# Three changes of order and engine in the attention stage of a two-block kernel

## The chip, the cores and the metric

The kernel runs on one core of a Trainium2 chip. The metric is the device time of one execution in microseconds; the times before are the median of three runs. A profile of one more execution gives the span from its first to its last instruction, and every instruction's start and duration.

## The reference

Two blocks follow each other. The first is linear attention with a decay, in blocks of 64 positions, over q, k and v of shape (batch 4, heads 8, length 768, width 64). The second mixes along the length with a low-rank pair U (768 x 32) and V (32 x 768), adds that to its input, and sends the sum through two dense layers with a relu between them. Cut to what matters:

```python
intra = einsum('bhic,bhjc->bhij', qb, kb) * Dmask      # decay mask
out   = einsum('bhij,bhjd->bhid', intra, vb) + einsum('bhid,bhde->bhie', qb * lam_pow, kv_state)
kv_state = lam_block * kv_state + einsum('bhsd,bhse->bhde', kb * rev_pow, vb)

x = out as (batch, 768, 512)
u = x + (x^T U V)^T                                     # low-rank sum along the length
y = u + relu(u w_ch1) w_ch2                             # 512 -> 2048 -> 512
```

U, V, w_ch1 and w_ch2 arrive as 64-bit floats; the kernel loads them as pairs of 32-bit words and makes 32-bit values of them itself.

## The kernel before

**Attention.** A step `s` handles 128 positions of one batch for all 8 heads; there are 6 steps in a batch and 24 in all, so the batches end with steps 5, 11, 17 and 23. In each step TensorE transposes q and k of the next step into one PSUM tile (`prep`, L358) that ScalarE copies out (L364). It multiplies k by q (`scores`, L406), VectorE multiplies the scores by the decay mask (`masked`, L415), and TensorE multiplies by v (`intra`, L444). TensorE also forms the new key-value product (`state`, L424), in the same PSUM buffer that `prep` uses, and VectorE takes it from there (L430 in a batch's first step, L432 in the later ones, there with ScalarE's faded old state, `fade`, L399). `inter` (L455) adds the part of the old state; ScalarE copies the step's result x out (L461). GpSimd scales q and k (`scale`, L390 and L379).

**The low-rank sum.** After the last step of a batch, TensorE sums U against the batch's six x tiles (`low`, L471) into a tile that shares its PSUM buffer with that of `intra`. ScalarE copies the sum out (L481). VectorE cuts it to its high bits (`low_rows`, L511). Three further pieces follow, each called by one `next_of_low`: `spread`, four ScalarE copies of the high part (L519); `low_part`, two subtractions that leave the low part (L523); `spread_low`, two ScalarE copies of that (L530). High and low parts stand in one tile, `p_hl`, in which TensorE multiplies them by V (`mix`, L551), first the high and then the low columns. VectorE adds the product to x, which makes it u (`mixed`, L563).

**u.** Seven steps after its own, u of a step is complete. It is stored to memory (`store`, L569, one transfer from the SP queue), transposed by TensorE (`turn`, eight L600), and split by VectorE (`split`, L620 and L621) into a high part t and a low part; `turned` lets ScalarE scale the high part (L607) and GpSimd form a third part (L608). The PSUM tile of the transposes is the one in which `mix` of the next step puts its product.

**The weights.** Conversions of U, V and the first two column tiles of w_ch1 from 64 to 32 bits are cut into small pieces (`weight_steps`, `split_steps`, `v_steps`). The dictionary `side` says in which step each piece is asked for, and `aside` runs those of a step: fetches on the SP queue, VectorE's L160, L149, L178, L186, L191, L209, L217 and L224, and ScalarE's L167, L168 and L212. ScalarE's pieces are put into a list that `late` runs in a later place. For V, VectorE's copies of the high part are L695 and the subtractions L699, one pair by VectorE and one pair by GpSimd.

**The order.** In this stage the order is written out by hand. The list `pieces` (L629 to L656) names the pieces of each step in order, and each piece issues its instructions to the queues of its engines, which take them strictly in that order. Nothing reorders them later. The number `done` is the step whose u is made in this step.

**After the attention.** The two dense layers follow as long rows of matrix products (L806, L816, then L939, L941, L943), each written as three products of high and low parts, with the last conversions and the transfers of the middle result beside them.

Of the kernel before, what the change touches and what calls it, by code (L numbers as in the profile page):

```python
# [18 lines left out]
def kernel(  # L19
# [28 lines left out]
    nc = tc.nc  # L48
# [3 lines left out]
    NT = S // P  # L52
# [10 lines left out]
    TG = N // P  # L63
# [5 lines left out]
    FG = (NS - NT - 1) // TG  # L69
# [11 lines left out]
    def on_scalar(what):  # L81
        if late and late[0] is None:
            late.append(what)
        else:
            what()
# [12 lines left out]
    def tmp(name):  # L98
        return wconv.tile([P, C], FP32, tag="tmp", bufs=3, name=name)
# [132 lines left out]
    def w1_steps(ft, in_parts=False, apart=False):  # L232
        def tile_of():
            w1v[ft] = w1_pool.tile([P, 3, C], F32R, tag="w1", name="w1")
            return w1v[ft]

        cols = moe_w_ch1[:, ft * P : (ft + 1) * P].rearrange("(c p) f -> p c f", p=P)
        return split_steps(tile_of, cols, in_parts, apart=apart)
# [244 lines left out]
    def low_rows(b):  # L483

        pp, t = pps.pop(b), tmp("p_h")[0:R]
        own = [(slice(g * R, (g + 1) * R), slice(g * P, (g + 1) * P)) for g in range(G)]
        if b == B - 1:
            h, h2, l, l2 = (p_hl[g * R : (g + 1) * R] for g in range(G))
            for rows, cols in own:
                nc.vector.tensor_scalar(  # L490
                    t[:, cols].bitcast(U32), pp[rows].bitcast(U32), HI, None, ALU.bitwise_and
                )

            def low_part():
                for rows, cols in own:
                    nc.vector.tensor_tensor(
                        out=l[:, cols], in0=pp[rows], in1=t[:, cols], op=ALU.subtract
                    )

            def spread():  # L500
                nc.scalar.copy(h, t)
                nc.scalar.copy(h2, t)

            def spread_low():
                nc.scalar.copy(l2, l.bitcast(FP32))

            pps[b] = [spread, low_part, spread_low]
            return

        rows_f = pp  # L510
        nc.vector.tensor_scalar(t.bitcast(U32), rows_f.bitcast(U32), HI, None, ALU.bitwise_and)  # L511
        wide = [slice(x * 2 * P, (x + 1) * 2 * P) for x in range(2)]

        def place(g, low):
            return p_hl[g * R : (g + 1) * R, wide[low]]

        def spread():
            for g in range(G):
                nc.scalar.copy(place(g, 0), t[:, wide[g // 2]])  # L519

        def low_part():
            for x in range(2):
                nc.vector.tensor_tensor(  # L523
                    out=place(2 * x, 1), in0=rows_f[:, wide[x]], in1=t[:, wide[x]],
                    op=ALU.subtract,
                )

        def spread_low():
            for x in range(2):
                nc.scalar.copy(place(2 * x + 1, 1), place(2 * x, 1).bitcast(FP32))  # L530

        pps[b] = [spread, low_part, spread_low]

    def next_of_low(b):
# [95 lines left out]
    for s in range(NS):  # L630
        b, c = divmod(s, NT)
        done = s - NT - 1
        more = s + 1 < NS
        turns = done > 0 and (done - 1) // TG < FG
        mixes = 0 <= done < NS - NT - 1
        step = [("prep", s + 1), ("scale", s + 1)] * more
        step += [("turn", done - 1)] * turns + [("mix", done)] * mixes
        step += [("mix", done + 1)] * (not more)
        step += [("next_of_low", b - 1)] * (c == 0 and b > 0)
        step += [("fade", s)] * (c == 1)  # L640
        step += [("late", s - 1)] * (s in (NT, 3 * NT - 1))
        step += [("split", done - 1)] * turns + [("next_of_low", b - 1)] * (c == 0 and b > 0)
        step += [("mixed", done)] * mixes + [("mixed", done + 1)] * (not more)
        step += [("next_of_low", b - 1)] * (c == 0 and b > 0)
        step += [("intra", s), ("state", s), ("inter", s)]
        step += [("late", s)] * (s < NT - 1 or s == NT)
        step += [("turned", done - 1)] * (done > 0) + [("late", s)] * (done >= 0)
        step += [("scores", s + 1)] * more
        step += [("low", b)] * (more and c == NT - 1)
        step += [("aside", s)] * (s >= 2 * NT)  # L650
        step += [("masked", s + 1)] * more
        step += [("low_rows", b)] * (more and c == NT - 1)
        step += [("fade", s + 1)] * (more and c > 0)
        step += [("aside", s)] * (s < 2 * NT)
        step += [("store", done)] * (done >= 0 and done // TG < FG)
        pieces += step  # L656
    waiting = {name: list(range(NS)) for name in "qkv"}

# [12 lines left out]
    def v_steps():  # L671

        st = {}

        def dst():
            if "v" not in st:
                st["v"] = wconv.tile([P, C], FP32, tag="wf", name="vf")[0 : 2 * R, 0:SH]
            return st["v"]

        def parts(gs):  # L680
            for half in range(2):
                rows, cols = slice(half * R, (half + 1) * R), slice(half * SH, (half + 1) * SH)
                for g in gs:
                    yield v_hl[g * R : (g + 1) * R, cols], rows

        def five():
            st["t"] = t = wconv.tile([P, C], FP32, tag="wt", name="vt")[0 : 2 * R, 0:SH]
            nc.vector.tensor_scalar(
                t.bitcast(U32), st["v"].bitcast(U32), HI, None, ALU.bitwise_and
            )  # L690
            on_scalar(lambda: high(0))

        def high(g, copy=nc.scalar.copy):
            for out, rows in parts((g,)):
                copy(out, st["t"][rows])  # L695

        def low(g, engine):
            for out, rows in parts((g,)):
                engine.tensor_tensor(  # L699
                    out=out, in0=st["v"][rows], in1=st["t"][rows], op=ALU.subtract  # L700
                )

        halves = [moe_V[:, half * SH : (half + 1) * SH] for half in range(2)]
        return weight_steps(dst, halves, SH, 2 * R, in_parts=True) + [
            five, lambda: low(1, nc.vector), lambda: high(2, nc.vector.tensor_copy),
            lambda: low(3, nc.gpsimd),
        ]
# [5 lines left out]
    side = {}  # L713
    for steps, at in (
        (u_side, (-1, 1, 1, 2, 2)),
        (v_steps(), (0, 0, 3, 3, 4, 4, 4, 5, 4, 5)),
        (w1_steps(0, True), (3, 4, 5, 6, 8, 9, 10, 11, 13, 14, 15)),
        (w1_steps(1, True, True), (8, 9, 10, 11, 16, 17, 19, 20, 21, 22, 23, NS)),
    ):
        assert len(steps) == len(at)  # L720
        for step, n in zip(steps, at):
            side.setdefault(n, []).append(step)
# [67 lines left out]
    turns = iter([0, 0, 0, 0] + [1, 0] * (NG * FT))  # L790
# [69 lines left out]
    c0, b = NS - NT, B - 1  # L860
# [182 lines left out]
```

## Time and profile before

| what | value |
|---|---|
| median of three runs | 676.49 us (675.99 to 676.75) |
| the profiled execution's own time | 676.67 us |
| its span | 674.9 us |
| TensorE busy | 659.7 us, 98% |
| VectorE busy | 500.4 us, 74% |
| ScalarE busy | 280.0 us, 41% |
| GpSimd busy | 111.9 us, 17% |
| attention steps | from the start to about 124 us |

The page gives the busy time of each engine (PE is TensorE, PEld its weight loads, DVE VectorE, ACT ScalarE, POOL GpSimd, SP the queue that issues transfers), the span in 40 slices with a digit for the busy tenths of each, the clock that TensorE was granted, and the chain of work that ended last. A line of the timeline has start, duration, engine, source line, operation, output and input, count, and in square brackets the idle time ahead of it with what ended it. A row of the list of waits has the waiting group, the group waited for, the total in us, the number of waits and the longest.

### The profile page before, as it was taken

The page shows a single profiled execution, that of the slowest core. Times are in us where ns is not written, and L with a number is a line of the kernel's source. Part 1 is how long each engine was busy: PE and PEld are TensorE (multiplying, and loading weights), DVE is VectorE, ACT ScalarE, POOL GpSimd, SP SyncE. Part 2 cuts the span into 40 slices and gives each one's busy share as a digit, 9 for nine tenths or more (in the row PEclk, how much of TensorE's full clock was granted, in tenths as well). Part 3 has the DMA queues.
Part 4 walks back from the last instruction along what each step waited for, and adds up shares of the span by engine and source line. Part 5 has one row for each costly group of instructions (what it writes and reads, how often), then busy time and mean ns, then how long its engine had stood idle before and what let it go on. Part 6 is the DMA issues. An engine that isn't in the chain of part 4 may idle for free.

```text
span 674.9 us, 13392 instructions
## 1 busy us (share of the span) xinstructions
PE 659.7 (98%) x5242; PEld 541.2 (80%) x5242; DVE 500.4 (74%) x864; ACT 280.0 (41%) x534; POOL 111.9 (17%) x92
## 2 busy tenths in 40 slices
PE   8989899999999999999999999999999999999997
PEld 7878788887888888888888888888888888888886
DVE  4778989887999777777798255786586776865864
ACT  3666777554555444444455122332232322322320
POOL 4446666440000000000000000030030200300300
PEclk9989999999999999999999999999999999999999
DMA  9999885164777655555577999945363363443421
GB/s 206 220 216 250 214 218 137 50 226 149 244 267 241 230 203 203 203 203 203 203 252 263 316 315 383 312 169 156 94 203 109 110 200 97 155 157 95 157 92 62
DMA packets 131776, 131.29 MB, mean 195 GB/s; under 512 B 81346, under 2 KB 89794, under 8 KB 131714
## 3 DMA queue, kind: packets, MB, share of 16 engines
q1 hardware_dynamic: 130512, 130.05, 60.8%
q8 instruction: 41, 0.67, 0.4%
q10 hardware_dynamic: 1202, 0.39, 0.2%
q14 instruction: 21, 0.17, 0.1%
HBM read 80.09 MB, written 50.33 MB: 193 GB/s over the span
## 4 chain that ended last, share of the span: by engine, by line
PE 93%; DVE 3%; issue 1%; SPq 1%; ACT 1%; DMA 1%; DVEq 0%
PE pz L806 27%; PE pz L941 13%; PE pz L939 13%; PE pd L816 13%; PE pd L943 13%; PE px L444 3%; PE pss L406 2%; PE px L455 2%; PE pqk L358 1%; PE pkv L424 1%; PE pp L471 1%; SPq L279 1%; DVE vp L523 1%; PE pm L551 1%; DMA qraw<-in_q_dram 1%
## 5 line engine op out<-in xcount | busy, mean ns | idle before, releaser
L806 PE MATMUL pz<-u_hl,w 128*128 128x512 f32 x768 | 190.1, 397 | 0.0
L806 PEld LDWEIGHTS pz<-u_hl,w 128*128 128x128 f32 x768 | 144.0, 188 | 35.2 <-ACT r L812 0.3
L941 PE MATMUL pz<-w_hl,m 128*128 128x512 f32 x384 | 151.1, 396 | 0.0
L939 PE MATMUL pz<-w_hl,m 128*128 128x512 f32 x384 | 150.9, 396 | 0.0
L943 PE MATMUL pd<-w_d,m 128*128 128x512 f32 x384 | 149.5, 396 | 0.0
L922 ACT ACTIVATE m<-mt 128x512 fp32r<-128x512 f32 x96 | 60.6, 632 | 196.3 <-PE pd L943 133.1
L923 DVE SCALAR_TENSOR_TENSOR m<-rm,m 128x512 fp32r<-128x512 f32 x96 | 71.5, 746 | 53.1 <-ACT m L922 52.6
L968 POOL TENSOR_TENSOR o<-o,u 128x512 f32<-128x512 f32 x20 | 29.9, 1528 | 447.4 <-DVE o L964 447.4
L821 DVE SCALAR_TENSOR_TENSOR r<-pd,r 128x512 f32<-128x512 f32 x96 | 61.8, 686 | 53.7 <-ACT r L812 43.5
L816 PE MATMUL pd<-u_d,w 128*128 128x512 f32 x384 | 98.6, 397 | 0.0
L812 ACT ACTIVATE r<-pz 128x512 f32<-128x512 f32 x96 | 52.2, 596 | 93.2 <-PE pz L806 93.1
L941 PEld LDWEIGHTS pz<-w_hl,m 128*128 128x128 f32 x384 | 72.3, 188 | 17.7
L939 PEld LDWEIGHTS pz<-w_hl,m 128*128 128x128 f32 x384 | 72.3, 188 | 17.6
L943 PEld LDWEIGHTS pd<-w_d,m 128*128 128x128 f32 x384 | 72.3, 188 | 17.6
L816 PEld LDWEIGHTS pd<-u_d,w 128*128 128x128 f32 x384 | 72.1, 188 | 17.3
L924 DVE SCALAR_TENSOR_TENSOR m<-m 128x512 fp32r<-128x512 f32 x96 | 69.1, 721 | 0.9
L921 DVE TENSOR_SCALAR mt<-rm 128x512 uint32<-128x512 uint32 x96 | 46.1, 481 | 27.1 <-DMA rm<-r_d 26.4
L415 DVE TENSOR_TENSOR sm<-pss,mask 128x512 f32<-128x512 f32 x48 | 30.8, 684 | 10.1 <-PE pss L406 10.0
L212 ACT CAST w<-wt 128x512 fp32r<-128x512 f32 x32 | 19.9, 621 | 30.5 <-DVE wt L209 23.4
L444 PE MATMUL px<-vraw,sm 128*64 128x64 f32 x768 | 29.3, 230 | 0.9 <-ACT faded L399 0.7
L390 POOL TENSOR_TENSOR qs<-qt,powq 128x512 f32<-128x512 f32 x20 | 26.1, 1306 | 23.2 <-ACT qt L364 22.4
L444 PEld LDWEIGHTS px<-vraw,sm 128*64 128x64 f32 x768 | 26.1, 141 | 4.3 <-ACT faded L399 0.9
(96 smaller groups left out, 677.1 us busy)
## 6 DMA issues: line engine op xcount, KB each, us to landing
r_d<-r SPq DMA_DIRECT2D x96, 256.0 KB, 2.5
rm<-r_d SPq DMA_DIRECT2D x96, 256.0 KB, 2.7
words<-in_moe_w_ch_dram SPq DMA_DIRECT2D x30, 512.0 KB, 4.2
w_d<-w SPq DMA_DIRECT2D x16, 768.0 KB, 3.3
w_hl<-w_d SPq DMA_DIRECT2D x16, 512.0 KB, 6.6
vraw<-in_v_dram SPq DMA_DIRECT2D x24, 256.0 KB, 4.1
u_d<-x_nat SPq DMA_DIRECT2D x24, 256.0 KB, 3.5
u<-u_d SPq DMA_DIRECT2D x24, 256.0 KB, 4.0
```

The lines of the kernel that those rows point to most:

```text
L444: nc.tensor.matmul(out=px[half[t], x, a, :], lhsT=sm[:, x, a, half[t]], rhs=vr[:, 2 * a + x, :], start=(a == 0), stop=(alone and a == HP - 1),
L806: nc.tensor.matmul(out=acc[g][0], lhsT=w[:, n, ct, :], rhs=uhl[g][:, n, ct, :], start=(ct == 0 and n == 0), stop=(ct == CT - 1 and n == 1),)
L812: nc.scalar.mul(rs[g], acc[g][0], 4096.0 + 1.0)
L816: nc.tensor.matmul(out=acc[g][1], lhsT=w[:, 2, ct, :], rhs=ud[g][:, ct, :], start=(ct == 0), stop=(ct == CT - 1),)
L821: nc.vector.scalar_tensor_tensor(rs[g], acc[g][1], 4096.0, rs[g], ALU.mult, ALU.add)
L921: nc.vector.tensor_scalar(t.bitcast(U32), r.bitcast(U32), HI, None, ALU.bitwise_and)
L922: nc.scalar.activation(out=m[:, 0], in_=t, func=AF.Relu)
L923: nc.vector.scalar_tensor_tensor(m[:, 1], r, 0.0, hi, ALU.max, ALU.subtract)
L924: nc.vector.scalar_tensor_tensor(m[:, 2], hi, E, low, ALU.mult, ALU.subtract)
L939: nc.tensor.matmul(out=pz, lhsT=m[:, 0, cols], rhs=hl[:, 0], start=first, stop=False)
L941: nc.tensor.matmul(out=pz, lhsT=m[:, 1, cols], rhs=hl[:, 1], start=False, stop=end)
L943: nc.tensor.matmul(out=pd, lhsT=m[:, 2, cols], rhs=dd, start=first, stop=end)
```

## The change

There are four edits, three of them in the list of pieces.

- `low_part` of batches 0 to 2 runs on GpSimd instead of VectorE.
- In the last step of batches 1 and 2 (steps 11 and 17, `early`), `store` and `turn` of the step's own u come ahead of `low`, and its `split` right behind `masked`. Before, `turn` and `split` came at the head of the next step. In the first step of a batch (`rows`), `scale` comes after `mix`, `spread` and `low_part`, and `spread_low` comes after `inter` and `turned` instead of before `intra`.
- From s = 7 on, `aside` comes ahead of `masked`. Before, it did so from s = 12.
- One piece of V's conversion, VectorE's copy of the high part (L695), moves from step 4 to step 5.

```diff
         def low_part():
             for x in range(2):
-                nc.vector.tensor_tensor(
+                nc.gpsimd.tensor_tensor(
                     out=place(2 * x, 1), in0=rows_f[:, wide[x]], in1=t[:, wide[x]],
                     op=ALU.subtract,
                 )
...
-        step = [("prep", s + 1), ("scale", s + 1)] * more
-        step += [("turn", done - 1)] * turns + [("mix", done)] * mixes
+        rows = c == 0 and b > 0
+        early = c == NT - 1 and more and done >= 0
+        step = [("prep", s + 1)] * more
+        step += [("turn", done - 1)] * (turns and not rows) + [("mix", done)] * mixes
         step += [("mix", done + 1)] * (not more)
-        step += [("next_of_low", b - 1)] * (c == 0 and b > 0)
+        step += [("next_of_low", b - 1)] * rows + [("next_of_low", b - 1)] * rows
+        step += [("scale", s + 1)] * more
         step += [("fade", s)] * (c == 1)
         step += [("late", s - 1)] * (s in (NT, 3 * NT - 1))
-        step += [("split", done - 1)] * turns + [("next_of_low", b - 1)] * (c == 0 and b > 0)
+        step += [("split", done - 1)] * (turns and not rows)
         step += [("mixed", done)] * mixes + [("mixed", done + 1)] * (not more)
-        step += [("next_of_low", b - 1)] * (c == 0 and b > 0)
         step += [("intra", s), ("state", s), ("inter", s)]
         step += [("late", s)] * (s < NT - 1 or s == NT)
         step += [("turned", done - 1)] * (done > 0) + [("late", s)] * (done >= 0)
+        step += [("next_of_low", b - 1)] * rows
         step += [("scores", s + 1)] * more
+        step += [("store", done), ("turn", done)] * early
         step += [("low", b)] * (more and c == NT - 1)
-        step += [("aside", s)] * (s >= 2 * NT)
+        step += [("aside", s)] * (s > NT)
         step += [("masked", s + 1)] * more
+        step += [("split", done)] * early
         step += [("low_rows", b)] * (more and c == NT - 1)
         step += [("fade", s + 1)] * (more and c > 0)
-        step += [("aside", s)] * (s < 2 * NT)
-        step += [("store", done)] * (done >= 0 and done // TG < FG)
+        step += [("aside", s)] * (s <= NT)
+        step += [("store", done)] * (done >= 0 and done // TG < FG and not early)
...
-        (v_steps(), (0, 0, 3, 3, 4, 4, 4, 5, 4, 5)),
+        (v_steps(), (0, 0, 3, 3, 4, 4, 4, 5, 5, 5)),
```

## The prediction

> **What bounds the kernel now.** I read the page first. TensorE is busy 98% of the span and makes 93% of the chain that ended last; its weakest slices all lie in the first fifth.
>
> ```profile
> span 674.9 us, 13392 instructions
> PE   8989899999999999999999999999999999999997
> PEclk9989999999999999999999999999999999999999
> PE 93%; DVE 3%; issue 1%; SPq 1%; ACT 1%; DMA 1%; DVEq 0%
> ```
>
> So only TensorE's idle time can be won. The busy times by stretches of 20 us put it: 16.98, 18.48, 17.34, 17.78, 19.66 and 18.42 us in the first six, 108.7 of 120 us, then 20.00 of 20 in each stretch from 140 on. Nearly all of its idle time, 11.3 us, lies in the attention steps. Second view, the waits between 40 and 230 us, longest first:
>
> ```profile
> PE pqk L358 <- DVE kv L430: 5.3, 3, 2.1
> ...
> PE pqk L358 <- DVE kv L432: 1.0, 1, 1.0
> ```
>
> Three waits of L358 for L430: one behind the low-rank sum of each of the batches 0, 1 and 2 (steps 7, 13, 19). The fourth, for L432, is in step 9. Third view, the timeline round the second of these:
>
> ```profile
> 66.58 1.52 PE L471 MATMUL pp<-x_nat,u_w 128*32 128x128 f32 x48
> 68.16 1.06 ACT L481 COPY p_f<-pp 32x128 f32<-32x128 f32 x4 [1.42 <-PE pp L471]
> 69.60 0.67 DVE L191 SCALAR_TENSOR_TENSOR wf<-m,sc 128x512 f32<-128x512 f32 x1
> 70.20 1.66 ACT L519 CAST vp<-p_h 32x256 fp32r<-32x256 f32 x4
> 71.37 1.05 POOL L379 TENSOR_TENSOR ks<-kraw,small 128x512 f32<-128x512 f32 x1
> 71.51 1.63 DVE L523 TENSOR_TENSOR vp<-p_f,p_h 32x256 fp32r<-32x256 f32 x2
> 72.79 0.85 ACT L530 CAST vp<-vp 32x256 fp32r<-32x256 f32 x2 [0.92 <-DVE vp L523]
> 73.78 0.41 DVE L430 COPY kv<-pkv 128x256 f32<-128x256 f32 x1
> 74.25 0.46 PE L358 MATMUL pqk<-ident,qraw 64*128 64x64 f32 x8 [2.06 <-DVE kv L430]
> 75.44 1.15 PE L444 MATMUL px<-vraw,sm 128*64 128x64 f32 x32
> ```
>
> L430 frees the bank that the next q and k transposes (L358) write. It is late because VectorE, in order, first does L191, the split of u (L620, L621), L523 and L563. The first L523 took 1.19 us, the second 0.42: the first stood behind GpSimd's L379. Fourth view, stretches of 1 us round the first boundary (columns: PE, PEld, DVE, ACT and POOL busy, granted clock, DMA share, GB/s):
>
> ```profile
> 41.00:42.00 1.00, 0.00 (x0) 0.00 (x0) 0.94 (x3) 0.89 (x3) 0.15 (x1) 1.00 0.26 59
> 42.00:43.00 1.00, 0.62 (x18) 0.62 (x18) 1.00 (x3) 0.89 (x2) 0.00 (x0) 0.91 0.96 248
> 43.00:44.00 1.00, 1.00 (x14) 0.78 (x14) 0.71 (x2) 0.69 (x2) 0.03 (x1) 0.50 1.22 275
> ```
>
> After the 1.70 us of idle there the clock stood at 0.50 from about 42.8 to 46.1. L444 took 1.97 us against 1.15, and L444 to the next L406 was 3.3 us against 2.2 in step 19: with the mix of u ahead of it the halving cost about 1.3 us.
>
> **What the Trainium skill says.** "SBUF — State Buffer", section "SBUF: two separate sides": VectorE (two SBUF inputs, or a two-port mode) and GpSimd share one port pair, an exclusive lock held for a whole instruction. The trace agrees: 1.19 against 0.42 us. "TensorE: Matmul & The Clock Gate", "What's actually happening": the clock is halved after an idle window of about 3.4 us that runs freely. The trace has 3.3 us at 0.50; but the idle of 2.06 and 1.58 us at the other boundaries did not trip it, so where idle time falls counts as well as its length. "GPSIMD Engine Reference", "Performance versus the Vector engine": GpSimd is some 2 times slower on two-input operations. Here 128x512 is 1.27 us (L390) against VectorE's 0.69.
>
> **Part 1: the low part by GpSimd.** The trace has no 32x256 instruction there; the nearest, L699 on GpSimd (32x384, the same subtraction), takes 1.01 to 1.09. By columns I take 0.70 each; bounds: 0.42 (VectorE's) and 1.27 (L390). VectorE loses 2 x 0.42 plus the lock's 0.8. GpSimd does the two first, then qs (1.27) and ks (1.05); at the second boundary it is ready at 69.95 and L390 then ends near 72.7, before inter at 75.7 needs it. ScalarE's order changes: L461 and L607 now stand ahead of the two L530.
>
> **Part 2: u's transposes ahead.** For u of steps 4 and 10 the eight L600 leave the head of the next step for the place ahead of L471. Eight of them hold up what follows by 0.24 (68.52 to 68.76), so L471 and all behind it is 0.24 later. L600 waits for L563, with L471 and so L481 queued behind it: L563 ended at 66.74 against the scores' end at 66.64, and with L186 gone from ahead of it (part 5) ends 0.6 earlier. Its L620 and L621 (0.7 each) then fill VectorE's idle 1.27 ahead of L511. The store's one DMA passes one weight fetch in SP's queue in step 11; neither is read within 20 us (the fetched words first at 91.79): nothing.
>
> **Part 3: the second and third boundary, summed.** From the start of L481, by the rows above: L364 at 1.09, L519 at 2.04, L461 at 3.72, L607 at 4.20, L530 at 4.75, its end at 5.60, and L551's last two matmuls and L444 at about 5.8 (5.7 to 6.0). GpSimd's part is done at 1.65 + 1.40 = 3.05: ahead of L530. L430 comes at about 3.0, so L358 no longer waits. What is late next is L530, in ScalarE's queue.
> - second: L481 at 68.16 + 0.24 = 68.40, L444 at 74.2 against 75.44: -1.2 (1.0 to 1.35).
> - third: L481 at 98.13 + 0.24 = 98.37, L444 at 104.2 against 104.93: -0.7 (0.5 to 0.9).
> Later steps follow rigidly: at the second boundary ScalarE ends L364 and L399 (1.07 each) at 74.0 + 2.1 = 76.1, and the next L461 is not due before TensorE's 76.4; L432 ends at 76.5, and the next L358 is due at 77.3; and from 124 on TensorE has no idle time that would take the gain up.
>
> **Part 4: the first boundary.** No u is ready, so no transposes move. But the new place 5 of V's copy (L695, two, 32x384) moves it from ahead of L415, where nothing waited, to ahead of L430. VectorE's queue at L511's end (38.11) is L699, L699, L695, L695, L430; GpSimd's is L523, L523, L390, L379, and the lock alternates as it did before. Ends: L699 38.67, L523 39.25, L699 39.65, L523 40.25, L695 40.45, L390 41.6, L695 41.8, L430 42.25, against 42.32: 0.0. If L695 passes twice in a row: -1.1 for L358, but L551 waits for L530 until 42.8, so -0.4; at 1.27 for each L523: +1.1. The halved clock: the idle time remains 1.6 to 1.7, so I leave it (else -1.3).
>
> **Part 5: conversions ahead of the masks, steps 8 to 11** (aside's place from s = 7; nothing is due at 7). L160 and L149 (0.4 each alone; L149 took 1.49 behind L390 at 54.04) fall into VectorE's idle 0.76 ahead of L415 at 52.50, which starts 0.15 later. L432 then comes at 55.9 instead of 57.45, and L358's wait of 1.0 goes. But L424 (60.41) writes the bank that L364 reads, and ScalarE runs from L461 at 55.93 through L607, L167, L168, four L399 and two L364 to 60.32 without a gap: unchanged. The wait moves to L424: 0.0 (+0.1 to -0.3). L178, L186 and L191, one each, lie in idle time of VectorE and cost nothing; without it 0.7 each. L191 leaves the place ahead of L620, which part 3 counts.
>
> **Sum**: -1.2 - 0.7 + 0.0 + 0.0 = -1.9 on the span of 674.9, that is 673.0; 1.8 lie around it, so 674.8 for the profiled execution's 676.67. That one stood 0.2 above the median of the runs: 674.6 us.
>
> **Rivals.**
> - The clock too: the first boundary's idle time no longer trips the halving: 674.6 - 1.3 = 673.3. For it: 1.58 did not trip, 1.70 did. Against: I find 1.64.
> - The gain is taken up: ScalarE, which I find the next limit, is later than summed (L461 to L607 was 0.61 at the boundaries, 0.48 elsewhere), or GpSimd at 1.27 adds 1.1 at the first boundary: a gain of some 0.8, 675.7. Within the 0.2% (1.35 us) that a measurement of this kernel can tell.
> - Slower: GpSimd's L523 takes far longer than its columns say. Each 0.1 us costs 0.2 in the first boundary's L430; from 1.75 each L530 waits too, at both others. The gain is gone at 1.65 each; at 2.3 it costs 3.2 + 1.0 + 1.0 less the 1.9 won: 679.8. Against: 1.09 was the most for half as many columns again.
> - Nothing moves: excluded for the order of instructions, which differs on all five queues.
>
> **How the numbers follow.** Forecast 0.45 (its own range 674.0 to 675.2), clock too 0.2, taken up 0.25, slower 0.1. Of the forecast 0.42 and all of the second are beyond 0.2%, and some of the third: faster 0.65, same 0.25, slower 0.1. The range reaches over the clock case below and the taken-up case above: 673.0 to 676.4.
>
> **What would show it.** Right: L358 no longer waits for L430 in steps 13 and 19, L551 waits there for L530, u's split stands ahead of L511, L523 on GpSimd is near 0.7, and L424 of step 10 is still at about 60.4. Wrong: L523 above 1.2; L444 of step 13 less than 0.8 earlier; or a stretch at half clock somewhere new, which would put up to 1.7 us against a gain of 1.9.

## The result, and the profile after

The changed kernel takes 674.32 us (median of 10 runs, 673.45 to 675.56) against 676.11 us of the kernel before on the same chip (10 runs, 674.03 to 676.75). The ratio is 0.9979, with a 95% interval of 0.9967 to 0.9991: wholly below 1, but on both sides of the 0.2% that the prediction took as its mark. The profiled execution took 673.84 us. These are its lines of the page that answer to those shown of before; line numbers of the code are unchanged up to the list of pieces and 5 higher behind it (L695 is L700 now, L699 is L704).

```profile
span 672.0 us, 13396 instructions
PE   8988999999999999999999999999999999999997
PEclk9999999999999999999999999999999999999999
PE 94%; DVE 2%; issue 1%; SPq 1%; ACT 1%; DMA 1%; DVEq 0%
```

The slice of the clock that stood at 8 is gone, and VectorE's share of the chain fell from 3% to 2%. Next, TensorE's own waits between 40 and 230 us, which is the whole list for that engine (the group, what it waited for, the total in us, the number, the longest):

```profile
PE pkv L424 <- issue: 1.8, 2, 1.3
PE pqk L358 <- DVE kv L430: 1.4, 1, 1.4
PE pm L551 <- DVE u_hl L621: 0.8, 2, 0.4
PE pm L551 <- ACT vp L530: 0.3, 1, 0.3
PE px L444 <- issue: 0.3, 1, 0.3
PE px L455 <- issue: 0.2, 1, 0.2
```

L358 waited three times for L430, 5.3 us in all; one wait of 1.4 is left, at the first boundary. The wait for L432 is gone, and L424 has one of 1.3 instead. New are two waits of L551 for u's split (L621), which I had not named, and one for L530, at the third boundary, which I had. At the second boundary the wait for L530 doesn't stand in the list; there it lies within L551's four products, which take 0.96 us from 71.58 on, against 0.48 at the same place before. The second boundary's timeline shows the order that this comes from:

```profile
66.40 1.06 ACT L481 COPY p_f<-pp 32x128 f32<-32x128 f32 x4 [1.70 <-PE pp L471]
...
66.61 0.69 DVE L621 TENSOR_TENSOR u_hl<-pm,ut 128x512 fp32r<-128x512 f32 x1
...
67.36 0.51 PE L551 MATMUL pm<-vp 64*128 64x256 f32 x4 [0.38 <-DVE u_hl L621]
...
68.06 1.52 POOL L523 TENSOR_TENSOR vp<-p_f,p_h 32x256 fp32r<-32x256 f32 x2 [1.98 <-DVE p_h L511]
...
69.99 0.42 DVE L430 COPY kv<-pkv 128x256 f32<-128x256 f32 x1 [1.36 <-PE pkv L424]
...
70.87 0.41 PE L358 MATMUL pqk<-ident,qraw 64*128 64x64 f32 x8
...
71.28 0.83 ACT L530 CAST vp<-vp 32x256 fp32r<-32x256 f32 x2
...
72.47 1.15 PE L444 MATMUL px<-vraw,sm 128*64 128x64 f32 x32
```

VectorE is early now: it idles 1.36 us before L430, and L358 has no bracket. From L481 to L444 it takes 6.07 us, where it took 7.28. I compare kernels by stretches, from one step's first L406 (the scores) to another's; a stretch without a boundary shows what varies for other reasons. Times in us from the two profiled executions, and from a repeat of the changed kernel:

| stretch, by the step whose scores start and end it | before | after | after, repeated |
|---|---|---|---|
| 6 to 8, with the first boundary | 13.07 | 11.63 | 11.60 |
| 8 to 12 | 18.49 | 19.04 | 18.50 |
| 12 to 14, second boundary | 12.13 | 11.16 | 11.16 |
| 14 to 18 | 17.85 | 18.45 | 17.85 |
| 18 to 20, third boundary | 11.64 | 11.16 | 11.15 |

The boundaries gave 1.44, 0.97 and 0.49. The first of these includes a full clock where before had a halved one. The changed kernel's profiled execution lost 0.5 in each of the two stretches between, in short pauses that have no releaser in the trace; the repeat does not have them, so they are not the change's.

### The profile page after: what moved, and what is told of

It is laid out like the page before. It is cut to its first block, busy times and chain, and to the rows that moved or that the text cites. A ratio compares the mean times of both kernels' runs of the same rounds, so it can differ in the third digit from the quotient of the medians.

```text
span 672.0 us, 13396 instructions
## 1 busy us (share of the span) xinstructions
PE 659.3 (98%) x5242; PEld 540.7 (80%) x5242; DVE 494.5 (74%) x858; ACT 280.3 (42%) x534; POOL 115.1 (17%) x98
## 4 chain that ended last, share of the span: by engine, by line
PE 94%; DVE 2%; issue 1%; SPq 1%; ACT 1%; DMA 1%; DVEq 0%
PE pz L811 27%; PE pz L946 13%; PE pz L944 13%; PE pd L821 13%; PE pd L948 13%; PE px L444 3%; PE pss L406 3%; PE px L455 2%; PE pkv L424 1%; PE pqk L358 1%; SPq L279 1%; PE pm L551 1%; PE pp L471 1%; DMA qraw<-in_q_dram 1%; PE pm L600 1%
## 5 line engine op out<-in xcount | busy, mean ns | idle before, releaser
L415 DVE TENSOR_TENSOR sm<-pss,mask 128x512 f32<-128x512 f32 x48 | 30.9, 685 | 12.1 <-PE pss L406 11.8
L444 PE MATMUL px<-vraw,sm 128*64 128x64 f32 x768 | 28.4, 226 | 1.1 <-issue 0.7
L406 PE MATMUL pss<-qt,kt 64*128 64x128 f32 x384 | 28.9, 291 | 0.0
L444 PEld LDWEIGHTS px<-vraw,sm 128*64 128x64 f32 x768 | 25.1, 138 | 4.3 <-issue 0.8
```

Of the source, the lines that this page charges most:

```text
L406: nc.tensor.matmul(out=pss[:, x, a, :], lhsT=kt[half[x], a, :], rhs=qt[half[x], a, :], start=True, stop=True,)
L444: nc.tensor.matmul(out=px[half[t], x, a, :], lhsT=sm[:, x, a, half[t]], rhs=vr[:, 2 * a + x, :], start=(a == 0), stop=(alone and a == HP - 1),
```

## The experiments

My theory: at the second and third boundary it is the order in the queues that counts, above all what stands ahead of L530 on ScalarE; VectorE has slack there. Rivals: what moved the time is VectorE's lighter load (L523 gone to GpSimd), or the transposes put ahead, or the earlier conversions, or the clock alone. Each set of runs has its own runs of the kernel before, with medians of 676.24 to 676.45 us. Where I give an execution's mean clock: one stretch of 3.4 us at 0.50 makes it 0.996 or 0.997 (so in six profiled executions), none leaves it at 0.999 or 1.0 (so in eight); that 0.994 or 0.995 is two such stretches follows by the same sum, but no trace shows it. I call such a stretch a fall of the clock.

The changed kernel itself has ratios of 0.9979 and 0.9971 in two sets of runs, so the times alone don't tell its variants apart where they differ by 0.001 or less. What is said of such differences rests on the stretches, each from one profiled execution; between the changed kernel and its repeat the second and third stretch agree to 0.01 us.

### The changed kernel again, and one part of it undone in each of three

**The same kernel again**, with a blank line in the source:

> The changed kernel once more, with nothing changed, as the measure for the other three and to see what of its profile repeats itself. Theory 1 (ScalarE's queue up to L530 now sets the second and third boundary): the stretch from the first L406 of the scores of step 12 to that of step 14 is 11.2 us again, that from step 18 to step 20 11.2 too, because nothing in them is left to chance. Stretches are named so below: second and third stretch; the first is step 6 to step 8 (11.6 in the profile of the changed kernel, 13.1 before). The idle times of TensorE that no semaphore explains (0.3 us each ahead of the end of L455 in steps 11, 16 and 17 of the changed kernel, 1.2 us in step 2 of the kernel before) should lie elsewhere or be gone if they have nothing to do with the change (theory A), or be at the same places if the change makes them (theory B). Time 674.3 us, 673.5 to 675.5.

674.27 us (22 runs), ratio to before 0.9971 (0.9960 to 0.9982); the stretches are in the table above. Of the 22 executions ten had a mean clock of 0.996 or 0.997 and a median of 675.1; that of the other twelve is 673.6. So the clock still falls in some executions of the changed kernel, and a fall costs about 1.5 us by these medians.

**L523 back on VectorE:**

```diff
-                nc.gpsimd.tensor_tensor(
+                nc.vector.tensor_tensor(
                     out=place(2 * x, 1), ...
```

> The changed kernel with the low part (L523) back on VectorE, all else as changed. Theory 1: at the second and third boundary VectorE has time to spare. L523 starts at L511's end, its second half stands behind L390 and ends some 1.8 us later, L563 and L430 follow, and L430 ends at about 70.8 where the scores ahead of L358 end at 71.0. Second and third stretch stay at 11.2 us. At the first boundary the queue of VectorE gets longer by 0.65 us, L358 waits 2.0 us instead of 1.4, and the clock is halved there in most executions: first stretch 12.3 at full clock, 13.6 with the halving. Whole: 0.6 to 1.9 us slower than the changed kernel, all of it in the first stretch. Theory 2 (VectorE's queue sets all three boundaries, and taking L523 off it is the gain): second and third stretch longer by 0.8 each, first by 1.6: 3 us slower than the changed kernel, that is, slower than before.

675.48 us, ratio 0.9994 (0.9979 to 1.0009). Second stretch 11.15, third 11.17: no loss. First stretch 13.82, with the clock halved. The second boundary of this kernel, from the timeline:

```profile
71.17 1.83 DVE L523 TENSOR_TENSOR vp<-p_f,p_h 32x256 fp32r<-32x256 f32 x2
...
73.64 0.41 DVE L430 COPY kv<-pkv 128x256 f32<-128x256 f32 x1
...
74.11 0.46 PE L358 MATMUL pqk<-ident,qraw 64*128 64x64 f32 x8 [0.46 <-DVE kv L430]
...
74.43 0.83 ACT L530 CAST vp<-vp 32x256 fp32r<-32x256 f32 x2
```

L358 does wait for L430 again, 0.46 us, but L530 ends only at 75.26 and L551 needs it, so that the wait costs nothing. GpSimd's part is worth something at the first boundary alone, where L358 waits 2.50 without it (1.70 in the repeat of the changed kernel with it). That wait is longer by 0.8 us, and falls of the clock are more frequent (seven executions of 14 with one, two with two, as against ten of 22 with one); at 1.43 us for a fall that makes some 1.3 us, as an estimate, where the median is 1.2 above the repeat's.

**The transposes, split and store of u back at the old place:**

```diff
-        early = c == NT - 1 and more and done >= 0
+        early = False
-        step += [("turn", done - 1)] * (turns and not rows) + [("mix", done)] * mixes
+        step += [("turn", done - 1)] * turns + [("mix", done)] * mixes
-        step += [("split", done - 1)] * (turns and not rows)
+        step += [("split", done - 1)] * turns
```

> The changed kernel with u's transposes, their split and the store of steps 11 and 17 back at their old place in the next step; the order of the low-rank sum's pieces, GpSimd's low part and the conversions stay as changed. Theory 1: the move costs time. L471 and L481 come 0.24 us earlier, with them all of ScalarE's queue up to L530, and L551 of the old product no longer waits for L621. L430 is due at about 70.2, ahead of the 71.0 at which L358 could start. Second and third stretch 10.9 us each: 0.5 us faster than the changed kernel. Theory 2: L620 and L621 behind L511 put 1.4 us back into VectorE's queue ahead of L430, L358 waits again: second and third stretch 11.7 to 11.9, 1.0 to 1.4 us slower than the changed kernel.

673.81 us, ratio 0.9961 (0.9944 to 0.9978), although its profiled execution had the clock halved. Second and third stretch 10.91 each, 0.25 less than in the changed kernel. The second boundary:

```profile
70.65 0.42 DVE L430 COPY kv<-pkv 128x256 f32<-128x256 f32 x1
...
71.17 0.41 PE L358 MATMUL pqk<-ident,qraw 64*128 64x64 f32 x8
...
72.63 0.80 PE L551 MATMUL pm<-vp 64*128 64x256 f32 x2 [0.37 <-ACT vp L530]
```

L430 ends at 71.07, and L358 again has no wait. So, with L523 on GpSimd, to put the transposes ahead is a loss by the stretches: it makes L481 0.24 us later, as worked out, and the time that the split leaves free on VectorE nobody needs. The two parts relieve VectorE twice: with L523 on VectorE and the split ahead, as in the run before this one, the boundaries were no slower either. No run takes both away and keeps the new places of `scale` and `spread_low`, so it isn't shown what these two are worth without any relief of VectorE.

**The conversions behind the masks again in steps 7 to 11:**

```diff
-        step += [("aside", s)] * (s > NT)
+        step += [("aside", s)] * (s >= 2 * NT)
...
-        step += [("aside", s)] * (s <= NT)
+        step += [("aside", s)] * (s < 2 * NT)
```

> The changed kernel with the conversions ahead of the masks only from step 12 on, as before. Theory 1: nothing changes. L358 of step 9 waits some 1.0 us for L432 again, but L424 of step 10 waits for ScalarE's L364 either way. From the scores of step 8 to those of step 12 it takes 19.0 us in the profile of the changed kernel (18.5 before), of which 0.3 to 0.5 are idle times that no semaphore explains; here 18.5 to 19.1. L191 stands between L511 and L563 again, which makes L430 of the second boundary 0.7 later, still ahead of L358: second stretch 11.2. Theory 2: that stretch of four steps gets longer by the wait of 1.0, and the second stretch by 0.7.

674.9 us, ratio 0.9975 (0.9965 to 0.9986). The stretch 8 to 12 is 18.50 with and without this edit: the wait only moves, as predicted. But the second stretch is 11.62, which the expectation does not have. The timeline ahead of that boundary has it:

```profile
64.10 0.75 DVE L186 SCALAR_TENSOR_TENSOR sc<-words,sc 128x512 uint32<-128x512 uint32 x1
...
66.10 0.68 DVE L563 TENSOR_TENSOR x_nat<-pm,x_nat 128x512 f32<-128x512 f32 x1
...
66.92 0.47 PE L600 MATMUL pm<-ident,x_nat 64*128 64x64 f32 x8 [0.24 <-DVE x_nat L563]
```

L186 is again ahead of the split and of L563, L563 ends at 66.78, and the transposes, which now stand ahead of L471, wait for it. L481 starts 3.39 us after the scores instead of 2.92. Part 2 of the prediction (the transposes ahead) makes TensorE wait for L563, and part 5 (the conversions ahead of the masks) brings L563's end forward; part 2 without part 5 costs 0.46 more at this boundary.

### ScalarE's order, V's copy, and the clock

**The two L530 ahead of L461 and L607:**

```diff
+        step += [("next_of_low", b - 1)] * rows
         step += [("intra", s), ("state", s), ("inter", s)]
...
         step += [("turned", done - 1)] * (done > 0) + [("late", s)] * (done >= 0)
-        step += [("next_of_low", b - 1)] * rows
```

> The changed kernel with the two L530 put ahead of L461 and L607 in ScalarE's queue, at all three boundaries; nothing else moves on any engine. Theory A (the order in ScalarE's queue up to L530 sets L444): L530 follows L519 directly, at about 70.1 and 99.7 instead of 71.28 and 100.88; L551 no longer waits for it, and L444 comes 0.45 (second) and 0.65 (third) earlier. But the two L364 behind are no earlier, since the same work stands ahead of them, and L424, which writes their bank, then waits for L364: L424 is only 0.2 earlier at each. Second and third stretch 10.95 each against 11.16, first 11.6 or a little less, time -0.4 against the changed kernel. Theory B (only the order matters, L424 waits for nothing): 10.7 and 10.5, time -1.1. Theory C (L530 does not hold TensorE at all): 11.16 and 11.16, time unchanged.

673.67 us, ratio 0.9961 (0.9948 to 0.9974), second and third stretch 11.00 and 11.01: theory A's size. Its second boundary:

```profile
70.00 0.83 ACT L530 CAST vp<-vp 32x256 fp32r<-32x256 f32 x2
...
71.49 1.01 PEld L444 LDWEIGHTS px<-vraw,sm 128*64 128x64 f32 x32 [0.30 <-ACT x_nat L461]
71.49 1.15 PE L444 MATMUL px<-vraw,sm 128*64 128x64 f32 x32
...
73.11 0.69 PE L424 MATMUL pkv<-vraw,ks 128*64 128x64 f32 x16 [0.47 <-ACT kt L364]
```

L551 no longer waits for L530, L444 starts 5.22 us after L481 (66.27) instead of 6.07, and L424 gives most of it back by its wait for L364. L530 was the limit for L444, and ScalarE's whole sum up to the second L364 is the next limit, 0.2 us behind. The wait of 0.30 of L444's weight loads (PEld) for L461 I had not foreseen.

**V's copy (L700) back at step 4**, the rest as changed:

```diff
-        (v_steps(), (0, 0, 3, 3, 4, 4, 4, 5, 5, 5)),
+        (v_steps(), (0, 0, 3, 3, 4, 4, 4, 5, 4, 5)),
```

> The changed kernel with V's copy L695 (L700 here) back at step 4, that is ahead of L415 in VectorE's queue and no longer ahead of L430. Theory A (my part 4: the copy, under the lock with GpSimd, is what keeps L430 late, and ScalarE's L530 at 41.07 to 41.9 is the next limit): L430 starts near 38.8, L358's wait of 1.4 at the first boundary goes, L551 waits for L530 instead, and L444 of step 7 starts at 42.2 against 42.27. First stretch 11.5 against 11.6 at full clock, time -0.1; what is idle is cut in two pieces by L358, so the halved clock should be no more frequent. Rival B (VectorE's queue alone sets this boundary): L444 near 41.3, first stretch 10.7, time -0.9. Rival C (the copy has nothing to do with L430): L430 stays at 40.75, nothing moves.

673.62 us, ratio 0.9964 (0.9951 to 0.9978). The first boundary of this kernel, and then that of the changed kernel (both from the timeline):

```profile
38.39 0.42 DVE L430 COPY kv<-pkv 128x256 f32<-128x256 f32 x1
...
39.14 0.41 PE L358 MATMUL pqk<-ident,qraw 64*128 64x64 f32 x8
...
40.53 0.83 ACT L530 CAST vp<-vp 32x256 fp32r<-32x256 f32 x2
...
40.98 0.81 PE L551 MATMUL pm<-vp 64*128 64x256 f32 x2 [1.01 <-ACT vp L530]
```

```profile
36.58 0.41 DVE L511 TENSOR_SCALAR p_h<-p_f 32x512 uint32<-32x512 uint32 x1 [1.28 <-ACT p_f L481]
...
37.03 1.55 DVE L704 TENSOR_TENSOR vp<-vf,vt 32x384 fp32r<-32x384 f32 x2
37.08 2.09 POOL L523 TENSOR_TENSOR vp<-p_f,p_h 32x256 fp32r<-32x256 f32 x2 [1.90 <-DVE p_h L511]
...
38.59 2.13 DVE L700 CAST vp<-vt 32x384 fp32r<-32x384 f32 x2
...
40.75 0.42 DVE L430 COPY kv<-pkv 128x256 f32<-128x256 f32 x1
...
41.23 0.46 PE L358 MATMUL pqk<-ident,qraw 64*128 64x64 f32 x8 [1.37 <-DVE kv L430]
```

With the copy ahead of L415, L430 comes 1.6 us after L511's end instead of 3.8, L358 does not wait, and L551 waits for L530 in its stead. The first stretch is 11.30 (theory A: 11.5; B: 10.7), 0.30 less than in the repeat of the changed kernel. None of its nine executions had a mean clock below 0.999, against ten below it of the repeat's 22. The kernel before, with its idle time filled and so at full clock, takes 11.64 for this stretch (the next two runs). So without V's copy the change would gain 0.34 there, and its fourth edit takes all but 0.04 of that back.

**The idle time filled, in the kernel before:**

```diff
-        step = [("prep", s + 1), ("scale", s + 1)] * more
+        step = [("busy", 5)] * (s == 7) + [("prep", s + 1), ("scale", s + 1)] * more
...
```

> The kernel before with five 128x128 matmuls of zeros (L343's) added at the head of step 7, in TensorE's queue right ahead of the L358 that waits 1.70 for L430; they compute nothing that is used and fill that idle time. Theory A (the idle of 1.70 there trips the halving, and the halving costs 1.3 to 1.4): the clock stays at 1.00 through the first stretch, which becomes 11.7 against 13.07; second and third stretch unchanged at 12.1 and 11.6; time 1.3 below the kernel before, 675.0, if most executions of the kernel before are halved. Rival B (the halving has another cause, such as the burst of transfers at 42 to 44): clock at 0.50 after 42.8 as before, first stretch 13.1, time as before or up to 0.3 more.

The profiled execution did as theory A has it: 1.38 us of L343 in the idle time, clock 1.00, first stretch 11.64. The transfers, rival B, are excluded as a cause by themselves: from 42 to 47 us they took a share of 1.08 to 1.13 here, at full clock, and 0.96 to 1.22 in the kernel before. The median did not do as theory A has it: 676.11 against 676.24 us, ratio 1.0000 (0.9987 to 1.0013), and ten of 14 executions had a mean clock of 0.997. So this kernel was run once more.

> The kernel of the filled idle time a second time, for its records: of its 14 executions ten had a mean clock of 0.997, although the profiled one had none halved up to step 19. Theory A (the halving goes to another idle place when the first is filled): in an execution at 0.997 the stretch at 0.50 lies behind the wait of 2.06 at the second boundary (about 74 to 78) or the 1.58 at the third. Rival B: it lies in the first stretch as before, filled or not. Rival C: it lies somewhere past the attention steps. If this execution is again without a halved stretch, nothing follows.

676.32 us, ratio 1.0005 (0.9994 to 1.0015); 13 of 18 executions at 0.996 or 0.997, the profiled one among them. Stretches of 1 us at its second boundary (busy of PE, PEld, DVE, ACT and POOL, granted clock, transfer share, GB/s):

```profile
72.00:73.00 1.00, 0.23 (x6) 0.23 (x8) 1.00 (x3) 0.95 (x3) 0.00 (x0) 1.00 0.47 108
73.00:74.00 1.00, 1.00 (x28) 0.98 (x24) 0.91 (x2) 0.83 (x2) 0.50 (x1) 0.81 1.18 321
74.00:75.00 1.00, 1.00 (x18) 0.80 (x16) 0.66 (x1) 1.00 (x4) 1.00 (x2) 0.50 0.60 180
```

The first stretch is again 11.64 at full clock, and now the second is 13.59 instead of 12.12: the halving has gone behind the wait of 2.06 at the second boundary and costs 1.47 there. Theory A holds in this execution: with one idle time filled, the halving came behind the next.

**The same five matmuls in the changed kernel**, at the head of its step 7:

> The changed kernel with the same five matmuls of zeros at the head of step 7, where L358 waits 1.37 for L430. Theory A (what halves the clock in some ten of 22 executions of the changed kernel is this idle time, and its boundaries two and three no longer have one that could): all executions at a mean clock of 0.999 or 1.0, the median as that of its undisturbed executions, 673.6 to 673.9, first stretch 11.6. Rival B (the halving only moves, as it seemed to in the kernel before): still a third or more of the executions at 0.997 and the median at 674.3.

673.69 us, ratio 0.9967 (0.9957 to 0.9978), first stretch 11.61, and all 21 executions at 0.999 or 1.0. In the changed kernel, then, the halving hangs on the first boundary's idle time and on no other in these runs. The median is 0.6 us below the repeat's, a difference that the two ratios (0.9967 and 0.9971) don't establish. Its list of waits also gives a name to the wait of step 10 that the changed kernel's list puts down to "issue":

```profile
PE pkv L424 <- ACT kt L364: 1.3, 1, 1.3
```

### One part alone

**Only L523 moved to GpSimd, in the kernel before:**

```diff
-                nc.vector.tensor_tensor(
+                nc.gpsimd.tensor_tensor(
                     out=place(2 * x, 1), ...
```

> The kernel before with one edit alone: L523 on GpSimd. With the old order of the step L523 stands behind L390 and L379 in GpSimd's queue. Theory A (the place in the queues decides, not which engine): at the second boundary L430 comes at 72.2 instead of 73.78 and L358 at 72.65 without a wait, but GpSimd reaches the two L523 only after L379, at 72.4, and ends them at 73.9; L530 ends at 74.75 instead of 73.64, and L551, which waits for it, lets L444 start at 75.1 against 75.44. Second and third stretch 11.8 and 11.3 (before 12.13 and 11.64); at the first boundary GpSimd is at L523 at 41.15 and L530 ends at 43.4, so 0.0 to 0.5 later there. Time as before, +-0.4. Rival B (VectorE's load was what held the boundaries): L444 1.2 and 0.9 earlier, stretches 10.9 and 10.7, time 674.2 or less.

677.18 us against 676.31, ratio 1.0012 (1.0000 to 1.0024): slower, if anything. First stretch 13.48 with the clock halved, second 12.38 (before 12.13), third 12.25 (before 11.64). The second boundary:

```profile
71.78 1.05 POOL L379 TENSOR_TENSOR ks<-kraw,small 128x512 f32<-128x512 f32 x1
...
72.51 0.41 DVE L430 COPY kv<-pkv 128x256 f32<-128x256 f32 x1
72.80 1.52 POOL L523 TENSOR_TENSOR vp<-p_f,p_h 32x256 fp32r<-32x256 f32 x2
...
74.80 0.38 PE L551 MATMUL pm<-vp 64*128 64x256 f32 x1 [0.41 <-ACT vp L530]
...
77.03 0.69 PE L424 MATMUL pkv<-vraw,ks 128*64 128x64 f32 x16 [0.46 <-ACT kt L364]
```

L430 comes 3.95 us after L481's start (68.56) instead of 5.62, as VectorE's load would have it, and yet it is no gain: L523 stands behind L390 and L379 in GpSimd's queue, L530 waits for it, and L551, L444 and L424 follow. Theory A's mechanism, but I had expected the stretches at 11.8 and 11.3; the waits of L444 for L461 and of L424 for L364, both behind the late L530 on ScalarE, were not in that sum. Together with L523 back on VectorE, above, this decides between the two: the new order without GpSimd gives both later boundaries in full, GpSimd without the new order gives none.

**The mix of steps 5 and 11 ahead of L358:**

```diff
-        step += [("turn", done - 1)] * (turns and not rows) + [("mix", done)] * mixes
+        step += [("turn", done - 1)] * (turns and not rows) + [("mix", done)] * (mixes and not rows)
...
-        step += [("low", b)] * (more and c == NT - 1)
+        step += [("low", b)] * (more and c == NT - 1) + [("mix", done + 1)] * early
```

> The changed kernel with the mix of steps 5 and 11 (four L551) put right behind L471 on TensorE, ahead of the two L358, so that it no longer stands behind u's split on VectorE, which reads the same bank (its wait of 0.38 for L621 at 66.98 to 67.36, which I had not foreseen). Nothing else moves. Theory A (that wait holds L444 of the boundary's step, but TensorE waits later for L530 anyway, whose time is set by ScalarE): L551's wait for L621 goes, L444 of the boundary's step comes about 0.3 earlier, the wait of L551 for L530 in the next step grows by as much, and the second and third stretch stay at 11.15, the time at 674.3. Rival B (the wait is on the path): both stretches 10.8, time -0.7.

674.44 us, ratio 0.9974 (0.9963 to 0.9984); second and third stretch 11.39 and 11.40. Both theories missed. L551 waits no more, but mix and split use one PSUM tile, and now the split waits for the mix. The second boundary:

```profile
67.16 0.69 DVE L620 TENSOR_SCALAR ut<-pm 128x512 uint32<-128x512 uint32 x1 [0.93 <-PE pm L551]
67.89 0.69 DVE L621 TENSOR_TENSOR u_hl<-pm,ut 128x512 fp32r<-128x512 f32 x1
68.49 0.41 DVE L511 TENSOR_SCALAR p_h<-p_f 32x512 uint32<-32x512 uint32 x1
...
68.93 1.66 ACT L519 CAST vp<-p_h 32x256 fp32r<-32x256 f32 x4
```

The split stands ahead of L511 on VectorE, so L519, and with it L530, is 0.24 us later. Of the two possible waits the one that I had overlooked was the cheaper.

### A better version

**What the runs above point to, together:** transposes back, V's copy back, L530 ahead of L461, and u's L607 and L608 of the boundary's step behind the two L364.

```diff
         step += [("scale", s + 1)] * more
+        step += [("turned", done - 2)] * (c == 1 and done > 1)
...
-        step += [("turned", done - 1)] * (done > 0) + [("late", s)] * (done >= 0)
+        step += [("turned", done - 1)] * (done > 0 and not rows) + [("late", s)] * (done >= 0)
```

> A combination meant to beat both: the changed kernel with the transposes, split and store of u back at their old place (as in the third of the earlier experiments), V's copy back at step 4, L530 ahead of L461 and L607, and u's L607 and L608 of the boundary's step behind the two L364 instead of ahead. Theory A (ScalarE's queue up to L530, then its L364, set the boundary): L444 and L424 both come 0.6 to 0.7 earlier than with the transposes back alone, where the stretches were 10.91: second and third 10.2 to 10.3; first 11.1 to 11.3 at full clock; time 672.1 to 672.6 against 674.3 of the changed kernel. Rival B (the rest of TensorE's idle at the boundaries comes from elsewhere): second and third stay at 10.9, time 673.8.

672.64 us (6 runs), ratio to before 0.9948 (0.9931 to 0.9965): faster than the kernel before, and probably than the changed one (0.9971, 0.9960 to 0.9982), though the intervals touch. No execution's mean clock was below 0.999. First stretch 11.16, third 10.12, as theory A has them. The second is 11.29, not 10.2. Up to L455 it agrees with the third to 0.01 us; then this profiled execution has a pause without a releaser in the middle of L455, like those in the table of the result:

```profile
74.43 0.69 PE L455 MATMUL px<-kv,qs 64*64 64x64 f32 x30 [0.84 <-issue]
```

## Why the prediction was right

The forecast was 674.6 us and "faster"; the median is 674.32. What removed the waits and what became the next limit was foreseen; that the total fits so closely is in part luck, as the part on the clock's share shows.

- **Part 3, the size of the gain.** Right in mechanism, a little high: -0.97 and -0.49 in place of -1.2 and -0.7, 1.46 for 1.9. L444 follows L481 by 6.07 at the second boundary where the sum had 5.8. Up to L607 the sum is right to 0.01 (4.21 after L481 for 4.20). Two of its terms are too small: L607 to L530 took 0.67 where it has 0.55, and from the end of L530 to L444 it took 0.36 where it has 0.2, because L551's last product starts only behind the second L530. To that extent the first half of the rival "taken up", a ScalarE that is later than summed, is what happened. That L530 "is late next", in ScalarE's queue, is shown by the runs with L530 moved ahead and with L523 back on VectorE.
- **Part 1.** L523 took 0.72 each without company (1.52 for two, with the gap between them) and 0.93 to 1.09 beside VectorE's L704, where I had 0.70 with bounds of 0.42 and 1.27. I credited GpSimd with clearing VectorE; the runs show that with the split ahead this is worth nothing at the later boundaries, because L551 waits for L530 anyway, and that alone it costs (0.25 and 0.61 us at these two).
- **Part 2.** The price of 0.24 on L481 is right (0.25 per boundary in the run with the transposes back). That they would fill VectorE's idle time is right, but of no use once L523 is on GpSimd. Not foreseen: the split ahead of the mix makes L551 wait 0.38 for L621. It lies within what TensorE later waits for L530 (without it, in the run with the transposes back, the boundary is shorter by L481's 0.24 and no more), and the run with the mix ahead shows that the other order is dearer.
- **Part 4, the waits.** Right: L430 started 3.76 us after L511's end, where the sum has 3.72 (from 38.11 to the start at 41.83), and at full clock the first stretch is 11.60 to 11.63 against 11.64 of the kernel before with its idle time filled. V's copy is what holds L430, as worked out.
- **Part 4, the clock.** Half wrong: I left the halving in, as a thing that is there or not. The runs show it as a thing of chance, in each execution anew. My reading that the 2.06 and 1.58 "did not trip it, so where idle time falls counts" came from a single execution; in the filled kernel the 2.06 did. (The halved stretch is also 3.4 us long, not 3.3: the clocks of its slices in the prediction's fourth view and the 0.50, 0.50 and 0.89 of those up to 47 give 42.8 to 46.2.)
- **The clock's share of the total.** Of all 174 executions of the kernel before in the four sets of runs, 56 had no fall, 95 one and 23 two, 0.81 each; of the changed kernel's 32, 20 had none and 12 one, 0.38 each. At 1.43 each (13.07 less 11.64) that is, as an estimate, 0.6 us that the change wins besides. 1.46 and 0.6 make 2.1, against 1.8 and 2.0 measured in the two sets. The times alone don't show the clock's share, since their intervals (0.6 to 2.2 us and 1.2 to 2.7 us) hold 1.5 as well as 2.1, and in executions without a fall the medians are 1.8 apart (675.4 of 21 of the kernel before, 673.6 of twelve of the repeat); it rests on the counts. By them, two errors of opposite sign cancelled in the total: 0.4 too much for the boundaries, 0.6 too little for the clock. That is luck. The rival "the clock too" was in the right direction, but seems to have named the wrong boundary: the first still has falls after the change, and what is gone are the idle times of 2.06 and 1.58 at the others. No trace of the kernel before itself shows a fall there; that of the kernel with the first idle time filled does, at the second.
- **Part 5.** Right: 0.0 in steps 8 to 11, the wait goes from L358 in step 9 to L424 in step 10 (at 57.93, 1.3 us, for L364). Right also, but only as an aside in part 2, is what it does bring: L563 in time for the transposes.
- **The rivals.** "Taken up" by L523 at 1.27 and "slower" by L523 above 1.65 are excluded by its 0.72 to 1.09. Where GpSimd does lose is its place behind L390 and L379, which the change avoids by calling `scale` later.

## What to carry to other kernels

To unburden the engine that a wait names is not enough: write down which instruction is late next, and whose queue it stands in; here it was L530 in ScalarE's, which made half of the relief of VectorE worthless. A piece handed to another engine comes as late as that engine's queue lets it, so the move and the order belong together. And an idle time of TensorE can cost more than its length, through the clock (here 1.4 us behind a wait of 1.70), in some executions and not in others: look at the mean clock of many runs, not at one profile.

## What the runs showed of the hardware

**The halved clock** came after idle times far below the length that the Trainium skill gives for it ("TensorE: Matmul & The Clock Gate", "What's actually happening": an idle window of about 3.4 us, which runs freely). It followed a wait of 1.70 in the kernel before, and one of 2.06 in the filled one; but the repeat of the changed kernel waited just as long, at full clock (its first boundary):

```profile
41.71 0.46 PE L358 MATMUL pqk<-ident,qraw 64*128 64x64 f32 x8 [1.70 <-DVE kv L430]
42.01 0.41 PE L358 MATMUL pqk<-ident,kraw 64*128 64x64 f32 x8
```

With L523 alone moved to GpSimd, waits of 0.70, 0.41 and 0.23 within 2.1 us stand ahead of the halved stretch, and 12 of 22 executions had at least one; with V's copy back, a wait of 1.01 (and one of 0.24 of the weight loads) gave none in nine. That chance decides would fit a window that runs freely, but these runs don't show it, nor how much idle time in it is enough. What the halving lasts, 3.4 us, agrees with the page's length of a window.

**Pauses without a releaser**, of 0.2 to 1.25 us, fall into TensorE's runs of small products (L358, L406, L444, L455) in some executions and not in others of the same program: 19.04 against 18.50 in one stretch, 18.45 against 17.85 in another. They are as large as a part of this change. Their cause stays open.
